# GpSimd additions ordered behind VectorE's in a scheduled attention and expert kernel, with new durations in its build-time scheduler

One core of a Trainium2 chip. The metric is the device time of one execution in microseconds (us), lower is better; a time below is a median over executions.

## The reference

Linear attention with a normalization per head gives a matrix x of 4608 rows by 512. Four experts follow, each a two-layer network with a ReLU, and their outputs are added with a weight per row. Everything is float32. Shortened:

```python
kv = einsum('bhsd,bhse->bhde', k, v)          # 8 batches, 8 heads, 576 rows, 64 columns
out = einsum('bhsd,bhde->bhse', q, kv)
x = out / sqrt(mean(out*out) + 1e-6) * g_norm # then laid out as 4608 x 512
p = domain_probs / (domain_probs.sum(-1, keepdims=True) + 1e-09)
for e in range(4):                            # w1: 512 x 1024, w2: 1024 x 512
    h = np.maximum(x @ w1[e], 0.0)
    out += p[:, e:e + 1] * (h @ w2[e])
```

## The kernel before

The rows go in nine blocks; a block and an expert make a stage, 36 in all. "Up" is x @ w1 with two nested levels of Strassen's scheme (7 products instead of 8, 49 in all), "down" is h @ w2, with one level or, in 18 "deep" stages, two. Strassen saves matmuls and costs additions. Those of PSUM banks are on VectorE and ScalarE; those of SBUF tiles ("port sums") may run on VectorE or on GpSimd:

```python
def combine(key, cost, out_, a, b, op, reads, writes):
    plan.add(
        key, cost,
        lambda eng: adder(eng).tensor_tensor(out=out_(), in0=a(), in1=b(), op=op),  # L337
        reads=reads, writes=writes, port=True,
    )
```

No order is written down. While the program is built, a list scheduler (`Plan.layout`) runs through a model of the core, with a duration for every operation. It decides which engine does a port sum, in which order each engine works, and which buffer a tile gets. It gives the SBUF port to one port sum at a time. A buffer is free again 0.3 us (`CROSS`) after the modelled end of its last use:

```python
op.end = busy[eng] = t + op.cost[eng]
if op.port:
    port = op.end
...
if b.left == 0 and b.kind is not None:
    end = max(o.end for o in [op] + b.readers + b.writers) + self.CROSS
    free[b.kind].append((end, b.slot))
```

On the chip only data and buffer waits remain of this; nothing holds the engines to the model's times. From the second expert on (but for the last stage), a result is added into the output in HBM by a store that GpSimd issues, planned at 0.9 us:

```python
def send(key, i):
    ...
    nc.gpsimd.dma_start(out=dst, in_=cell(i)[parts, :], accum_op=ALU.add)   # L936
    ...
    plan.add(
        key, {"POOL": 0.9 * len(where)} if e and not again else {"SP": 0.55 * len(where)},
        fn, ..., holds=[acc[i // 2]],
    )
```

Of the kernel before, what the change touches and what calls it, by code (L numbers as in the profile page):

```python
# [211 lines left out]
def kernel(  # L212
# [98 lines left out]
    plan = Plan()  # L311

    def pe(products, columns, passes=2):
        return {"PE": passes * products * (2 * columns + 6) / 2400 + 0.003}

    def dve(n):
        return {"DVE": 0.17 + 0.00108 * n}

    def act(n):
        return {"ACT": 0.19 + 0.00088 * n}  # L320

    def either(n):
        return {"DVE": 0.17 + 0.00108 * n, "POOL": 0.1 + 0.0025 * n}

    def gp(n):
        return {"POOL": 0.1 + 0.0025 * n}

    SPC = {"SP": 0.55}

# [64 lines left out]
    def weights_1(e, key, step, need):  # L394
# [11 lines left out]
        def form(k_, o, a, b, op):  # L406
            corner[o] = Buf(None, f"w1c_{e}_{o}")
            combine(
                k_, either(1024), lambda: f[o].ap[:], lambda: f[a].ap[:], lambda: f[b].ap[:], op,
                [f[a], f[b], corner[a], corner[b]], [f[o], corner[o]],  # L410
            )
# [6 lines left out]
        for j, m in enumerate(OUTER):  # L418
            x, low, y = f[m], corner[m], Buf("w1y", f"w1y_{e}_{m}")
            parts = {}  # L420
            for n, (uq, kt) in ((1, (0, 0)), (2, (0, 1)), (7, (1, 0)), (4, (1, 1))):
                parts[n] = (
                    [x, low] if n == 7 else [x],
                    lambda x=x, uq=uq, kt=kt: two(x.ap[:])[:, kt, uq * HN:(uq + 1) * HN],
                )
            for n, at in ((5, 0), (6, 1), (3, 2)):
                parts[n] = ([y], lambda y=y, at=at: y.ap[:, at * HN:(at + 1) * HN])
            for o, a, b, op in (
                (5, 7, 4, ALU.add), (7, 1, 7, ALU.subtract), (6, 5, 1, ALU.subtract),
                (3, 2, 6, ALU.subtract),  # L430
            ):
                combine(
                    need + j / 7, either(HN), parts[o][1], parts[a][1], parts[b][1], op,
                    parts[a][0] + parts[b][0], [low] if o == 7 else [y],
                )
            w1f[e][m] = parts

    def weights_2(e, key, step, deep):
# [9 lines left out]
        def form(k_, o, a, b, op):  # L448
            combine(
                k_, either(1024), lambda: f[o].ap[:], lambda: f[a].ap[:], lambda: f[b].ap[:], op,  # L450
                [f[a], f[b]], [f[o]],
            )
# [37 lines left out]
    def scaled(key, name, raw, n, x):  # L490
# [4 lines left out]
        def rows(b):  # L495
# [6 lines left out]
        )  # L502
        plan.add(
            key, dve(NT),
            lambda eng: nc.vector.reduce_sum(out=ss.ap[0:n, :], in_=rows(sq), axis=AX.X),
            reads=[sq], writes=[ss],
        )

        def power(eng):
# [8 lines left out]
        plan.add(key - 0.3, {"POOL": 1.9}, power, reads=[ss], writes=[ss, rt])  # L518
        plan.add(
            key, dve(NT),  # L520
            lambda eng: nc.vector.tensor_tensor(
                out=rows(x), in0=rows(raw),
# [5 lines left out]
    def attention(b, key, span, rem):  # L528
# [3 lines left out]
        for hp in range(NPAIR):  # L532
# [26 lines left out]
            def turn(eng, bank=bank, qt=qt):  # L559
                for r in range(NR):  # L560
                    rs = slice(r * P, (r + 1) * P)
                    nc.tensor.transpose(bank.ap[:, rs], qt.ap[:, rs], ident[:])  # L562

            plan.add(at(hp), pe(4, P, 1), turn, reads=[qt], writes=[bank])
            plan.add(
                at(hp), act(NT),
# [15 lines left out]
            def diagonal(eng, bank=bank, to=kvbd[hp]):  # L582
                for r in range(2):
                    rows = slice(r * D, (r + 1) * D)
                    nc.scalar.activation(out=to.ap[rows, rows], in_=bank.ap[rows, 0:D], func=ACT.Copy)

            plan.add(at(hp), pe(12, D), key_values, reads=[kt, vt], writes=[bank])
            plan.add(at(hp), {"ACT": 0.5}, diagonal, reads=[bank], writes=[kvbd[hp]])

            raw = Buf("ab" if b else "db", f"raw{n}")  # L590

            def attend(eng, raw=raw, qT=qT, kb=kvbd[hp]):
                for r in range(NR):
                    rs = slice(r * P, (r + 1) * P)
                    nc.tensor.matmul(raw.ap[:, rs], lhsT=qT.ap[:, rs], rhs=kb.ap[:])  # L595

            plan.add(at(hp + 0.4), pe(4, P), attend, reads=[qT, kvbd[hp]], writes=[raw])
            x = Buf("small", f"x{n}")
            scaled(at(hp + 0.4), n, raw, P, x)
# [172 lines left out]
    def up(s, e, views):  # L772
# [16 lines left out]
        for i, m in enumerate(OUTER):  # L789
# [4 lines left out]
            for j, mm in enumerate(ORDER):  # L794
# [28 lines left out]
                def total(a, t, src, add_, whole=whole, key=key):  # L823
                    plan.add(
                        key - 0.4, dve(HN),
                        lambda eng: nc.vector.tensor_tensor(  # L826
                            out=block(whole, a, t), in0=src.ap[:, 0:HN], in1=add_.ap[:], op=ALU.add),
                        reads=[src, add_], parts=[whole],
                    )
# [338 lines left out]
    with tc.manual_schedule(engines={ENG.PE, ENG.DVE, ENG.Activation, ENG.Pool, ENG.SP}):  # L1168
        for i in range(P // D):
            nc.sync.dma_start(out=gcol[i * D:(i + 1) * D, :], in_=g_norm.unsqueeze(1))  # L1170
        make_identity(nc, ident[:])
        nc.vector.memset(mhalf[:], -0.5)
        nc.vector.memset(bd_home[:], 0.0)
        for op in order:
            op.fn(op.eng)


# [26 lines left out]
```

## Time and profile before

| | before |
|---|---|
| median of all its first runs | 1797.2 us (1792.6 to 1798.3) |
| span of the profiled run | 1793.0 us |
| busy TensorE, VectorE, ScalarE, GpSimd | 98%, 66%, 46%, 54% |
| time that is not matmul pace | about 65 us |

A busy share of 98% hides what matters here, since the pace of the matmuls, as the prediction works it out, comes to 1728 us only, and the page counts 1760 as busy. The views to read are the waits of TensorE and the granted clock, which the prediction quotes.

### The profile page before, as it was taken

The numbers are of one execution on the slowest core, as the hardware profiler recorded it, in microseconds if no ns is written. First come the engines' busy times: TensorE is split into PE (matmuls) and PEld (weight loads), VectorE is DVE, ScalarE is ACT, GpSimd is POOL, SyncE is SP. The second block draws the span as 40 slices with busy tenths as digits, with TensorE's granted clock in tenths as the row PEclk, the third lists the DMA queues.
The fourth block names the chain that finished last, engine by engine and source line by source line (L and its number), as shares of the span: only waits on it lengthen the run. The fifth ranks groups of instructions, "written<-read, shape, count | busy, mean of one in ns | idle before, by whom it ended". The sixth has DMA issues, their size and how long they took to land.

```text
span 1793.0 us, 36253 instructions
## 1 busy us (share of the span) xinstructions
PE 1760.0 (98%) x14138; PEld 1683.6 (94%) x14138; DVE 1177.1 (66%) x1909; ACT 815.9 (46%) x1913; POOL 973.0 (54%) x816
## 2 busy tenths in 40 slices
PE   8999999999999999999999999999999999999998
PEld 8899999999989899999999899999999899999997
DVE  5864664556665677777774677777774767777754
ACT  3544544444333345555543345555543345555541
POOL 4945554555335546666546536666555636666520
PEclk9999999999999999999999999999999999999999
DMA  9854544532333334444564334444465334444441
GB/s 238 238 158 145 169 142 124 174 101 112 142 125 107 87 95 111 111 106 106 142 158 118 93 97 106 107 107 107 107 174 135 97 100 107 106 107 107 108 117 36
DMA packets 148587, 220.79 MB, mean 123 GB/s; under 512 B 49600, under 2 KB 90816, under 8 KB 148416
## 3 DMA queue, kind: packets, MB, share of 16 engines
q1 hardware_dynamic: 133312, 191.21, 35.0%
q0 software_dynamic: 15104, 27.27, 10.1%
q8 instruction: 111, 1.82, 0.4%
q14 instruction: 60, 0.49, 0.1%
HBM read 145.30 MB, written 73.14 MB: 122 GB/s over the span
## 4 chain that ended last, share of the span: by engine, by line
PE 84%; POOL 5%; DMA 5%; DVE 3%; issue 2%; ACT 1%; SPq 1%; DVEq 0%; POOLq 0%; ACTq 0%
PE u L802 38%; PE db L966 18%; PE db L1039 9%; PE ab L1039 8%; PE ab L966 6%; DMA out_dram<-big 4%; POOL big L337 4%; DVE big L337 2%; PE ab L595 1%; PE ab L577 1%; POOL out_dram L936 1%; PE ab L605 1%; PE ab L562 1%; SPq L343 1%; DVE big L1072 1%
## 5 line engine op out<-in xcount | busy, mean ns | idle before, releaser
L802 PE MATMUL u<-xf,big 128*128 128x128 f32 x3600 | 494.4, 276 | 0.8 <-ACT snap L818 0.6
L826 DVE TENSOR_TENSOR big<-u,snap 128x256 f32<-128x256 f32 x675 | 280.6, 422 | 305.6 <-PE u L802 201.7
L818 ACT ACTIVATE snap<-u 128x256 f32<-128x256 f32 x756 | 289.6, 384 | 387.9 <-PE u L802 319.8
L802 PEld LDWEIGHTS u<-xf,big 128*128 128x128 f32 x3600 | 456.9, 192 | 9.3 <-ACT snap L818 1.2
L337 POOL TENSOR_TENSOR big<-big,big 128x256 f32<-128x256 f32 (+1 forms) x181 | 295.8, 1638 | 206.5 <-DVE big L337 107.8
L337 DVE TENSOR_TENSOR big<-big,big 128x1024 f32<-128x1024 f32 (+1 forms) x330 | 379.1, 1160 | 32.1 <-ACT big L785 14.5
L802 PE MATMUL u<-xf,w1y 128*128 128x128 f32 x2700 | 381.1, 277 | 11.5 <-DVE big L826 10.3
L802 PEld LDWEIGHTS u<-xf,w1y 128*128 128x128 f32 x2700 | 342.8, 192 | 17.9 <-DVE big L826 11.5
L966 PE MATMUL db<-big,big 128*128 128x256 f32 x1336 | 316.8, 381 | 0.0
L966 PEld LDWEIGHTS db<-big,big 128*128 128x128 f32 x1336 | 242.4, 191 | 26.8
L785 ACT ACTIVATE big<-big 128x1024 f32<-128x1024 f32 x130 | 136.6, 1052 | 20.6 <-DVE big L337 18.1
L936 POOL DMA_DIRECT2D out_dram<-big x98 | 90.3, 1003 | 90.2 <-ACT big L913 45.6
L1064 ACT ACTIVATE snap<-db 128x256 f32<-128x256 f32 x216 | 76.9, 356 | 118.3 <-PE db L1039 105.2
L818 ACT ACTIVATE big<-u 128x256 f32<-128x256 f32 x225 | 86.2, 383 | 95.4 <-PE u L802 84.2
L1072 DVE TENSOR_TENSOR big<-ab,snap 128x256 f32<-128x256 f32 (+1 forms) x204 | 78.8, 386 | 70.9 <-PE ab L1039 40.3
L913 ACT ACTIVATE big<-db,p_all 128x256 f32<-128x256 f32 x96 | 45.5, 474 | 130.2 <-PE db L966 130.2
L337 POOL TENSOR_TENSOR big<-big 128x512 f32<-128x512 f32 (+1 forms) x53 | 74.5, 1406 | 44.5 <-ACT big L785 23.2
L1100 POOL TENSOR_TENSOR big<-big 128x512 f32<-128x512 f32 x17 | 36.2, 2131 | 113.2 <-ACT snap L818 113.2
L337 DVE TENSOR_TENSOR big<-big 128x512 f32<-128x512 f32 (+1 forms) x70 | 93.7, 1342 | 0.2 <-POOL big L337 0.2
L1039 PE MATMUL db<-big,big 128*128 128x128 f32 x648 | 89.8, 275 | 0.0
L920 DVE SCALAR_TENSOR_TENSOR big<-db,p_all,big 128x256 f32<-128x256 f32 x75 | 36.2, 482 | 75.6 <-PE db L966 75.5
L966 PE MATMUL ab<-big,big 128*128 128x256 f32 x360 | 85.8, 384 | 0.0
(198 smaller groups left out, 2682.4 us busy)
## 6 DMA issues: line engine op xcount, KB each, us to landing
xf<-x SPq DMA_DIRECT2D x108, 512.0 KB, 3.7
out_dram<-big POOLq DMA_DIRECT2D x82, 256.0 KB, 5.6
xf<-x_h SPq DMA_DIRECT2D x81, 256.0 KB, 3.1
xf<-x SPq DMA_DIRECT2D x81, 256.0 KB, 3.2
x<-xf SPq DMA_DIRECT2D x36, 512.0 KB, 3.7
big<-in_moe_w_dram SPq DMA_DIRECT2D x31, 512.0 KB, 5.1
small<-in_q_dram SPq DMA_DIRECT2D x72, 128.0 KB, 4.2
kv<-in_k_dram SPq DMA_DIRECT2D x30, 288.0 KB, 3.3
```

The source lines that it names most:

```text
L337: lambda eng: adder(eng).tensor_tensor(out=out_(), in0=a(), in1=b(), op=op),
L785: lambda eng: nc.scalar.activation(out=b.ap[:], in_=b.ap[:], func=ACT.Relu),
L802: nc.tensor.matmul(ps.ap[:, u * P:(u + 1) * P], lhsT=w1f[e][m][mm][1]()[:, u * P:(u + 1) * P], rhs=views[m][mm][1](), start=(mm in (1, 2, ...
L818: lambda eng: nc.scalar.activation(out=where(), in_=ps.ap[:, 0:HN], func=ACT.Copy),
L826: lambda eng: nc.vector.tensor_tensor(out=block(whole, a, t), in0=src.ap[:, 0:HN], in1=add_.ap[:], op=ALU.add),
L913: lambda eng: nc.scalar.activation(out=cell(i, half), in_=ap(), func=ACT.Copy, scale=prob()),
L920: lambda eng: nc.vector.scalar_tensor_tensor(out=cell(i, half), in0=ap(), scalar=prob(), in1=cell(i, half), op0=ALU.mult, op1=ALU.add,),
L936: nc.gpsimd.dma_start(out=dst, in_=cell(i)[parts, :], accum_op=ALU.add)
L966: nc.tensor.matmul(ps.ap[:, 0:HN], lhsT=four(h[m])[:, kt // 2, t, kt % 2, :], rhs=w2f[e][m].ap[:, kt * HN:(kt + 1) * HN], start=(m in (1, ...
L1039: nc.tensor.matmul(ps.ap[:, o * P:(o + 1) * P], lhsT=b.ap[:, col:col + P], rhs=w2q[e][m][mm][1]()[:, kt, :], start=(mm in (1, 2, 5) and o ...
L1064: lambda eng: nc.scalar.activation(out=where(), in_=group_of(ps.ap), func=ACT.Copy),
L1072: lambda eng: nc.vector.tensor_tensor(out=cell(tq, dq), in0=group_of(src.ap), in1=group_of(add_.ap), op=ALU.add,),
```

## The change

The intent: in the model, port sums of VectorE and GpSimd take turns; on the chip, GpSimd runs ahead of the order and holds the port while VectorE needs it. So each GpSimd port sum gets a wait for the last VectorE port sum ahead of it (the "rule"). The scheduler's durations are also set to what the trace shows. All of it:

```diff
     def pe(products, columns, passes=2):
-        return {"PE": passes * products * (2 * columns + 6) / 2400 + 0.003}
+        return {"PE": passes * products * (0.008 + 0.0008125 * columns) + 0.003}
     def dve(n):
-        return {"DVE": 0.17 + 0.00108 * n}
+        return {"DVE": 0.185 + 0.00104 * n}
     def either(n):
-        return {"DVE": 0.17 + 0.00108 * n, "POOL": 0.1 + 0.0025 * n}
+        return {"DVE": 0.185 + 0.00104 * n, "POOL": 0.15 + 0.00225 * n}
     def gp(n):
-        return {"POOL": 0.1 + 0.0025 * n}
+        return {"POOL": 0.15 + 0.00225 * n}
...
+        held = None
         for op in order:
-            op.fn(op.eng)
+            made = op.fn(op.eng)
+            if op.port and op.eng == "DVE":
+                held = made.ins.name
+            elif op.port and op.eng == "POOL" and held is not None:
+                tc.add_manual_dep(made.ins, held, mybir.DependencyInfo(
+                    mybir.DependencyClass.Sync, mybir.DependencyReason.DATA
+                ), reason="SBUF port")
```

## The prediction

> **What bounds the kernel now.** Four experts run over nine blocks of rows, 36 stages; each multiplies by w1 (up) and w2 (down), both by nested Strassen sums, so that VectorE and GpSimd do many additions of SBUF tiles (L337, L1100: "port sums" below) beside TensorE. Deep down stages are those with a second Strassen level. I read the page's busy shares first, then TensorE's waits, then the timeline around the longest of them, then the clock there.
>
> On the page: the span, the busy time of each engine, and the two largest groups of the first matrix product and its eviction.
>
> ```profile
> span 1793.0 us, 36253 instructions
> PE 1760.0 (98%) x14138; PEld 1683.6 (94%) x14138; DVE 1177.1 (66%) x1909; ACT 815.9 (46%) x1913; POOL 973.0 (54%) x816
> ...
> L802 PE MATMUL u<-xf,big 128*128 128x128 f32 x3600 | 494.4, 276 | 0.8 <-ACT snap L818 0.6
> L826 DVE TENSOR_TENSOR big<-u,snap 128x256 f32<-128x256 f32 x675 | 280.6, 422 | 305.6 <-PE u L802 201.7
> ```
>
> TensorE is busy in 98% of the span, so it sets the pace. What matters is how much of its time is not matmul pace. The chain of work shows the pace: 24 passes of 128 columns in 2.68 us (0.1117 us each) and 16 passes of 256 columns in 3.46 us (0.216 us each). The source gives the passes: 36 up stages of 49 products, 2 matmuls, 2 passes are 7056; the 18 deep down stages have 18 x 49 x 2 x 2 = 3528 more of 128 columns; the other 18 have 18 x 14 x 4 x 2 = 2016 of 256; attention and filler add 706 of 128 and 832 of 64 columns (24 in 0.92 us, 0.038 each). So (7056 + 3528 + 706) x 0.1117 + 2016 x 0.216 + 832 x 0.038 = 1261 + 435 + 32 = 1728 us. Of the 1793 us, only about 65 are not pace. That bounds every gain at 3.6%, and head and tail are in it: TensorE is idle 9.1 of the first 100 us, and the last matmul starts 5.4 us before the end.
>
> The waits of TensorE, by what ended them (total us, times, longest), those on VectorE:
>
> ```profile
> PE u L802 <- DVE big L826: 10.5, 6, 3.0
> PE ab L1039 <- DVE big L1072: 6.2, 11, 0.9
> ...
> PE u L802 <- DVE small L826: 0.6, 1, 0.6
> ...
> PE ab L1039 <- DVE small L1072: 0.4, 1, 0.4
> ```
>
> They sum to 10.5 + 6.2 + 0.6 + 0.4 = 17.7 us. L826 and L1072 are the evictions that add a PSUM bank and a snapshot: matmuls wait because VectorE has not emptied a bank. VectorE is busy 66% of the span and its evictions take their normal 0.42 us, so the question is what stood ahead of them. The timeline at the longest such wait (start, duration, engine, line, operation; GpSimd is POOL):
>
> ```profile
> 993.13 1.29 POOL L337 TENSOR_TENSOR kv<-big,kv 128x256 f32<-128x256 f32 x1
> ...
> 996.71 1.11 POOL L337 TENSOR_TENSOR x_rem<-x_rem,small 128x256 f32<-128x256 f32 x1
> ...
> 998.08 1.09 POOL L337 TENSOR_TENSOR x_rem<-small,x_rem 128x256 f32<-128x256 f32 x1
> 1000.19 0.74 DVE L826 TENSOR_TENSOR big<-u,snap 128x256 f32<-128x256 f32 x2
> ...
> 1000.98 1.16 PE L802 MATMUL u<-xf,w1y 128*128 128x128 f32 x4 [3.05 <-DVE big L826]
> ```
>
> and the chain of waits in the same place (start, duration, what):
>
> ```profile
> 993.46 6.81 DVE big L337
> 1000.26 0.68 DVE big L826 x2
> ```
>
> A VectorE sum of 128x1024 took 6.81 us, where the median of its form is 1.22. GpSimd ran eight 128x256 sums from 993.13 without a pause, and the VectorE sum finished only after the last of them; the eviction behind it started at 1000.2 and TensorE stood 3.05 us. The same picture is at 604 and 1405, at the other two changes of expert. Then the clock (us, busy of PE, PEld, DVE, ACT, POOL, granted clock, DMA share, GB/s):
>
> ```profile
> 997.60:1001.00 3.40, 0.35 (x4) 0.16 (x3) 3.33 (x3) 0.75 (x2) 1.57 (x3) 1.00 0.09 37
> 1001.00:1004.50 3.50, 3.50 (x13) 3.14 (x14) 1.82 (x3) 0.00 (x0) 0.00 (x0) 0.51 0.37 117
> 1004.50:1010.00 5.50, 5.50 (x40) 5.19 (x39) 1.48 (x4) 2.46 (x6) 2.58 (x3) 1.00 0.06 22
> ```
>
> After the stall, 3.5 us ran at clock 0.51. The lost time is 3.5 x 0.49 = 1.7 us for each of the three, 5.1 in all. A smaller form comes once in each of 15 deep down stages:
>
> ```profile
> 771.41 4.21 DVE L337 TENSOR_TENSOR small<-big 128x512 f32<-128x512 f32 x1
> ...
> 772.02 2.98 POOL L337 TENSOR_TENSOR big<-big,big 128x1024 f32<-128x1024 f32 x1
> ```
>
> A 0.68 us sum took 4.21, ending 0.6 us after the GpSimd sum of 1024 finished at 775.0. The 11 waits of L1039 on L1072 (6.2 us) follow these.
>
> **What the Trainium skill says.** "SBUF — State Buffer", section "Who interferes with whom": VectorE and GpSimd share one port pair, held as an exclusive lock for a whole instruction; a VectorE operation with two SBUF inputs contends with a GpSimd operation that reads SBUF, and the later one blocks fully. The trace agrees in kind (1.22 becomes 6.81), and goes further: eight GpSimd sums in a row kept VectorE out, so it did not get in between two of them. "GPSIMD Engine Reference", section "Instruction dispatch", puts a two-input body at about 2.5 cycles per element; at the 1.2 GHz that "Trainium Kernel Development and Optimization" gives, 1024 elements would take 2.13 us plus overhead, and the lower half of the trace's 1024 sums takes 2.34 to 2.36. "TensorE: Matmul & The Clock Gate", section "Why this matters for your kernels", warns of TensorE idle gaps over about 3 us between bursts, which drop the clock; the three half-clock stretches in the middle of this run all follow gaps of about 3.1 us. "Perfetto Trace Analysis", section "GPSIMD Engine Instruction", says to time GpSimd by start-to-start spacing: the eight sums are recorded at 1.1 us each but start 0.68 us apart.
>
> **The change, part by part.** It makes every GpSimd sum that uses the port wait for the VectorE sum ahead of it in the build's order. VectorE never waits for GpSimd on this account. So it prevents overtaking, and nothing else. I paired the port sums of the trace with the build order: 735 on VectorE, 618 on GpSimd. 311 of the 618 GpSimd sums started before the VectorE sum ahead of them had ended (144 even before it had started), by 715 us summed, 2.3 on average. The VectorE sums took 135 us more than the medians of their sizes (0.28, 0.42, 0.68, 1.23 us for 128, 256, 512, 1024). In 134 us of this I can name the last GpSimd sum in the way: in 101 it stood later in the order (85 cases), which the change forbids, in 33 earlier (59 cases), which it does not touch. Of the 22 blocks over 2 us, 20 are of the forbidden kind, among them the three long ones and the 15 of 3.5 us.
>
> Gain: 17.7 us of waits plus 5.1 of half clock is 22.8 us; the forbidden kind is 75% of the blocked time (101 of 134) and 91% of the long blocks (20 of 22); I choose 85%, 19 us.
>
> Cost: the 311 sums get later. GpSimd has room: its sums at unblocked pace are 103 x 2.36 + 124 x 1.27 + 316 x 0.73 + 75 x 0.46 = 666 us, with 111 of DMA issue and 83 of the two attention operations 860; the 715 us of waiting, if it all came on top, gives 1575 of 1793. What it makes late was not wanted early, since the order planned it after the VectorE sum; but trains behind a wait can hold the accumulating stores and the attention powers in the same queue. I put 2 us on TensorE for that, an estimate without a row behind it.
>
> The new durations change no work, but reshuffle the order on every engine. The number of port sums stays 1353; GpSimd gets 90, 150, 293, 84 of 1024, 512, 256, 128 (before: 103, 124, 316, 75). At the same pace this is 655 us against 666, and VectorE's sums 612 against 607. Filler in the head falls from 65 to 62 pairs. Neither engine sets the pace, so I count zero with some 5 us of scatter.
>
> Sum: 1796.7 - 19 + 2 = 1780 us, 0.9% less.
>
> **Rivals.** (1) GpSimd becomes the bound: its sums form the weights and inputs of the next stage, and one waiting too long starves TensorE. For: GpSimd already waited 127 us on L337 of VectorE in 45 waits of up to 7.1 us, and would wait more. Against: no wait of TensorE in the trace was ended by a GpSimd sum. It would give 1800 to 1830. (2) The block only changes sides. The new order still has trains of up to seven GpSimd sums between two VectorE sums at the expert changes; started later than before, they can meet the VectorE sum behind them, which has no wait. At 0.68 us each that is 4.8 us again, and a TensorE stall. For: 33 us of such blocks exist now. Against: the order keeps evictions between, paced by TensorE. If it keeps the stalls, 1790 to 1800. (3) All waits on VectorE vanish and more of the small gaps with them: 1796.7 - 23 - 5 = 1769.
>
> **Range and chances.** I predict 1780 us, 1766 to 1793 in 8 of 10. Over 2% faster is below 1760.7, a loss of 36 of the 65 us that are not pace, where I can name 23: 6%. Over 2% slower is above 1832.6 and needs rival 1 in force: 3%. Within 2%: 91%.
>
> **What would show it.** Right: no VectorE sum of 1024 over some 4 us, no 512 of 4.2; TensorE's waits on L826 and L1072 below 4 us together; no half clock at the expert changes; more idle time of GpSimd ended by VectorE's L337. Wrong: TensorE's waits ended by GpSimd sums or by matrix forms, or long VectorE sums with the GpSimd sum ahead of them in the order, or a head longer by several us.

## The result, and the profile after

The changed kernel took 1789.3 us (1788.1 to 1790.1, 4 runs) against 1797.2. The ratio is 0.996, interval 0.9941 to 0.9979. The gain is 7.9 us, where 1796.7 - 1780 = 16.7 was predicted: less than half.

The page after (span, busy time by engine, the same group of evictions; columns as in the prediction):

```profile
span 1786.8 us, 36290 instructions
PE 1753.4 (98%) x14132; PEld 1677.8 (94%) x14132; DVE 1140.3 (64%) x1910; ACT 817.5 (46%) x1913; POOL 831.4 (47%) x815
...
L826 DVE TENSOR_TENSOR big<-u,snap 128x256 f32<-128x256 f32 x720 | 298.7, 421 | 293.1 <-PE u L802 205.0
```

VectorE fell from 1177.1 to 1140.3 us and GpSimd from 973.0 to 831.4. Their work is nearly the same (by the prediction's count 5 us more of sums on VectorE and 11 less on GpSimd), so most of this is blocked time that is gone. Pairing the port sums with the order again, no GpSimd sum of the 617 starts before the VectorE sum ahead of it has ended (before: 311 of 618). But not all blocking is gone. VectorE's port sums still take 86 us more than the medians of their sizes, where it was 135. All of it that can be named is now of the kind that the change doesn't touch, behind GpSimd sums that stand earlier in the order: 85 us in 180 cases, where it was 33. Only one of these is over 2 us. The timeline at the first change of expert that the prediction showed:

```profile
994.20 0.72 POOL L337 TENSOR_TENSOR kv<-kv,small 128x256 f32<-128x256 f32 x1 [1.33 <-DVE big L337]
...
998.40 1.23 DVE L337 TENSOR_TENSOR big<-big,big 128x1024 f32<-128x1024 f32 x1
...
999.76 0.73 POOL L337 TENSOR_TENSOR x_rem<-big,x_rem 128x256 f32<-128x256 f32 x1 [1.43 <-DVE big L337]
```

The GpSimd sums now take 0.72 us instead of 1.1, the VectorE sum of 1024 takes 1.23 instead of 6.81, and the GpSimd sum after it waits 1.43 us for it. TensorE does not stop. Around the three changes of expert (busy of PE, PEld, DVE, ACT, POOL, then clock, DMA share, GB/s):

```profile
600.00:620.00 20.00, 20.00 (x135) 18.74 (x134) 11.48 (x19) 7.75 (x17) 7.68 (x10) 1.00 0.43 106
985.00:1010.00 25.00, 25.00 (x167) 23.35 (x166) 13.60 (x22) 10.35 (x22) 18.58 (x27) 1.00 0.42 110
1395.00:1420.00 25.00, 25.00 (x172) 23.50 (x171) 13.44 (x23) 9.48 (x22) 18.28 (x25) 1.00 0.44 110
```

TensorE is busy throughout at clock 1.00. So the three stalls with their half clock, 14.3 us by the prediction's count (3 x 3.05 + 5.1), are gone as predicted. Where did half of that go? The waits of TensorE (total us, times, longest):

```profile
PE ab L1039 <- DVE big L1072: 10.1, 15, 0.7
PE ab L605 <- DVE small L521: 6.4, 4, 4.7
PE u L802 <- ACT snap L818: 4.7, 9, 1.2
...
PE u L802 <- DVE big L826: 0.9, 2, 0.6
PE u L802 <- DVE small L826: 0.8, 1, 0.8
```

L826 fell from 11.1 to 1.7 us. But L1072 rose from 6.2 to 10.1, with 15 waits instead of 11; waits on the snapshot copies L818 of ScalarE rose from 1.1 to 4.7; and L521, a part of the attention, rose from 2.4 to 6.4, nearly all in one wait of the head (the first 100 us or so, where the attention starts). Together these are (10.1 - 6.6) + 3.6 + 4.0 = 11 us given back, against 11.1 - 1.7 + 5.1 = 14.5 won. That leaves 3.5 of the 6.2 us between the two profiled spans; the rest lies in gaps too short for these rows, and I cannot assign it. The chain of waits in one deep stage (start, duration, what):

```profile
725.66 4.53 DMA out_dram<-big
...
730.28 0.42 DVE big L337
...
732.52 0.42 DVE big L1072
...
732.98 1.16 PE ab L1039 x8
```

A store from `big` to the output lands, and only then can a small VectorE sum run. Behind it VectorE does an eviction L826 and a sum of 1024, which the cut leaves out, and then the eviction L1072, for which TensorE waits 0.70 us. The sum of 1024 in the timeline:

```profile
731.14 1.45 DVE L337 TENSOR_TENSOR big<-big,big 128x1024 f32<-128x1024 f32 x1
```

It takes 0.22 us more than its median of 1.23, beside a GpSimd sum of 0.71 us that started at 730.79. So the port has at most a small part in this wait; the store comes first.

### The profile page after: what moved, and what is told of

The parts are those of the page before. It is cut to its first block, busy times and chain, and to the rows that moved or that the text cites. A ratio compares the mean times of both kernels' runs of the same rounds, so it can differ in the third digit from the quotient of the medians.

```text
span 1786.8 us, 36290 instructions
## 1 busy us (share of the span) xinstructions
PE 1753.4 (98%) x14132; PEld 1677.8 (94%) x14132; DVE 1140.3 (64%) x1910; ACT 817.5 (46%) x1913; POOL 831.4 (47%) x815
## 4 chain that ended last, share of the span: by engine, by line
PE 85%; DMA 6%; POOL 4%; DVE 2%; issue 2%; SPq 0%; ACT 0%; DVEq 0%; POOLq 0%; ACTq 0%
PE u L802 38%; PE db L966 18%; PE db L1039 9%; PE ab L1039 8%; PE ab L966 6%; DMA out_dram<-big 4%; POOL big L337 3%; DVE big L337 1%; PE ab L595 1%; PE ab L577 1%; PE ab L605 1%; POOL out_dram L936 1%; PE ab L562 1%; PE ab L644 0%; DMA out_dram<-small 0%
## 5 line engine op out<-in xcount | busy, mean ns | idle before, releaser
L802 PE MATMUL u<-xf,big 128*128 128x128 f32 x3600 | 503.0, 276 | 5.8 <-ACT snap L818 4.7
L826 DVE TENSOR_TENSOR big<-u,snap 128x256 f32<-128x256 f32 x720 | 298.7, 421 | 293.1 <-PE u L802 205.0
L802 PEld LDWEIGHTS u<-xf,big 128*128 128x128 f32 x3600 | 462.2, 192 | 17.1 <-ACT snap L818 7.5
L337 DVE TENSOR_TENSOR big<-big,big 128x1024 f32<-128x1024 f32 (+1 forms) x377 | 431.3, 1159 | 40.4 <-ACT big L785 15.6
L818 ACT ACTIVATE snap<-u 128x256 f32<-128x256 f32 x756 | 289.5, 384 | 362.1 <-PE u L802 263.8
L802 PE MATMUL u<-xf,w1y 128*128 128x128 f32 x2700 | 378.4, 275 | 0.0
L802 PEld LDWEIGHTS u<-xf,w1y 128*128 128x128 f32 x2700 | 340.4, 192 | 2.1
L337 POOL TENSOR_TENSOR big<-big,big 128x256 f32<-128x256 f32 (+1 forms) x174 | 238.3, 1374 | 151.7 <-DVE big L337 65.0
L966 PE MATMUL db<-big,big 128*128 128x256 f32 x1280 | 302.8, 380 | 0.0
L966 PEld LDWEIGHTS db<-big,big 128*128 128x128 f32 x1280 | 231.3, 190 | 25.3
L818 ACT ACTIVATE big<-u 128x256 f32<-128x256 f32 x240 | 92.1, 384 | 114.6 <-PE u L802 106.8
L337 POOL TENSOR_TENSOR big<-big 128x512 f32<-128x512 f32 (+1 forms) x81 | 95.5, 1184 | 69.0 <-DVE big L337 54.1
L1072 DVE TENSOR_TENSOR big<-ab,snap 128x256 f32<-128x256 f32 x216 | 83.2, 385 | 51.0 <-PE ab L1039 33.8
L337 POOL TENSOR_TENSOR small<-big,small 128x128 f32<-128x128 f32 (+1 forms) x46 | 28.8, 625 | 127.2 <-DVE big L337 68.0
L1039 PE MATMUL db<-big,big 128*128 128x128 f32 x616 | 86.3, 275 | 0.0
L1039 PE MATMUL ab<-kv,big 128*128 128x128 f32 x500 | 74.7, 278 | 10.1 <-DVE big L1072 10.1
```

The source lines that it names most:

```text
L802: nc.tensor.matmul(ps.ap[:, u * P:(u + 1) * P], lhsT=w1f[e][m][mm][1]()[:, u * P:(u + 1) * P], rhs=views[m][mm][1](), start=(mm in (1, 2, ...
L818: lambda eng: nc.scalar.activation(out=where(), in_=ps.ap[:, 0:HN], func=ACT.Copy),
L826: lambda eng: nc.vector.tensor_tensor(out=block(whole, a, t), in0=src.ap[:, 0:HN], in1=add_.ap[:], op=ALU.add),
L966: nc.tensor.matmul(ps.ap[:, 0:HN], lhsT=four(h[m])[:, kt // 2, t, kt % 2, :], rhs=w2f[e][m].ap[:, kt * HN:(kt + 1) * HN], start=(m in (1, ...
L1039: nc.tensor.matmul(ps.ap[:, o * P:(o + 1) * P], lhsT=b.ap[:, col:col + P], rhs=w2q[e][m][mm][1]()[:, kt, :], start=(mm in (1, 2, 5) and o ...
L1072: lambda eng: nc.vector.tensor_tensor(out=cell(tq, dq), in0=group_of(src.ap), in1=group_of(add_.ap), op=ALU.add,),
```

## The experiments

All ten gave correct results. Each was timed in 5 rounds against the kernel before, which had medians of 1795.5, 1796.5 and 1795.5 us in the three jobs. Runs 1 and 2 split the change, and have exactly the instruction order, on every engine, of the kernel before and of the changed one.

### 1. The rule alone

Edit: the loop of the change, without the new durations.

> The rule alone: the durations of before, so each engine's order is that of before, and only the new waits are added. Theory A (the rule is worth what I predicted, and the order that the new durations make gives part of it back): the three stalls of 3.05 us and their half clock (14.3 us together) and most of the 6.6 us of waits on L1072 go, less about 3 us at the head: 1779 us, and the waits of TensorE on L1072 below 2 us. Rival B (the rule takes with one hand and gives with the other: what it makes late in the deep down stages and the head costs TensorE some 8 us, and the order is neutral): 1789 us, as with the whole change, with waits on L1072 of 6 us or more.

Measured: 1778.5 us, ratio 0.9904 (0.9891 to 0.9918). The time is Theory A's, to half a us. But its second half fails. The waits of TensorE and of VectorE in this run, and one VectorE row of its timeline:

```profile
PE ab L1039 <- DVE big L1072: 8.6, 11, 1.2
```

```profile
DVE big L1072 <- DMA out_dram<-big: 51.4, 12, 4.8
```

```profile
773.77 0.42 DVE L1072 TENSOR_TENSOR big<-ab,snap 128x256 f32<-128x256 f32 x1 [4.79 <-DMA out_dram<-big]
```

No VectorE sum of 512 takes over 2.3 us now, and still L1072 holds TensorE up for 8.6 us instead of 6.2. VectorE, freed of its 3.5 us block, arrives earlier and waits 4.79 us for a store. So the port's block was not what bound this place. The profile before had said so. This is its chain of waits at the place that the prediction read in the timeline:

```profile
771.46 6.84 DMA out_dram<-big
...
778.42 0.42 DVE big L1072
...
780.17 1.16 PE ab L1039 x8
```

The store, 6.84 us from issue to landing, releases L1072 at 778.4; the port block ended at 775.6, inside the same wait. What made up for it in run 1: no wait on L826 is left but one of 0.2 us.

### 2. The new durations alone

Edit: the three changed lines of durations, without the loop.

> The new durations alone: each engine's order is that of the changed kernel, without the waits of the rule. Theory A (the order costs): 1802 to 1806 us, with the three stalls at the changes of expert still there and stalls of 0.87 us at L1039 in the 15 deep down stages. Rival B (the order is neutral): 1795 to 1799.

Measured: 1793.5 us, ratio 0.999 (0.9978 to 1.0003). Near Rival B by the time, though the order is not neutral. Its waits of TensorE:

```profile
PE ab L1039 <- DVE big L1072: 10.3, 15, 0.7
PE ab L605 <- DVE small L521: 6.2, 4, 4.5
PE ab L659 <- DVE small L521: 3.2, 1, 3.2
PE u L802 <- DVE big L826: 3.1, 4, 1.1
...
PE u L802 <- ACT snap L818: 1.1, 4, 0.5
```

This order, without any rule, already has short stalls on L826 (3.1 us instead of 10.5, the longest 1.1) and no half clock after the head: the trains (GpSimd sums in a row) are still there, with VectorE sums of 5.2 us at 995 and 1404, but TensorE waits only 1.1 us behind each. The order pays with 10.3 us on L1072, and with waits of 4.5 and 3.2 us in the head. So the long stalls can be removed once only, and the rule had little left to win here: 1793.5 to 1789.3. The waits on the snapshots are 1.1 us here and 4.7 with the rule: those are the rule's, in this order.

### 3. The rule without the head

Edit, on the changed kernel: the wait is made only where `op.key > 1.5`.

> The changed kernel, with the rule left out of the first stage and a half (keys up to 1.5). If the 4.67 us wait of TensorE for the attention power (GpSimd queue held by a sum that waits for VectorE) is the rule's doing, it falls to below 2 us and the time to 1786 us. If it comes from the new order (three VectorE sums of 1024 ahead of the reduction), the wait stays above 4 us and the time at 1789.

Measured: 1798.5 us, ratio 1.0013 (1.0 to 1.0027). A miss. The long wait of the head stays, and a second one comes:

```profile
PE ab L605 <- DVE small L521: 6.2, 4, 4.5
PE ab L659 <- DVE small L521: 3.3, 1, 3.3
```

The first is therefore the order's, as run 2 agrees (4.5). The second, 3.3 us, is one that the rule prevents. The waits on the snapshots are 7.2 us here, and the head has 3.4 us more at half clock, at 75.8. So in this order the rule does two things: outside the head it makes the kernel some 5 us slower (1793.5 in run 2, 1798.5 here, with intervals of the ratios that just touch), and in the head it is worth some 9 us (1798.5 to 1789.3). The timeline of the changed kernel shows the first: a GpSimd sum waits for VectorE, the power (L514) comes after it, then the scaling L521, then the transposes L605:

```profile
56.91 0.73 POOL L337 TENSOR_TENSOR big<-big 128x256 f32<-128x256 f32 x1 [2.63 <-DVE big L337]
...
59.53 1.70 POOL L514 TENSOR_TENSOR rt<-ss,mhalf 128x8 f32<-128x8 f32 x1
...
62.01 1.12 PE L605 MATMUL ab<-ident,small 128*128 128x128 f32 x4 [4.67 <-DVE small L521]
```

Without the wait of the rule at 56.91 the end was the same, so the wait was not what decided it.

### 4. The rule for one kind of sum

Edit, on the kernel before: the rule only where `op.outs[0].kind == "w2y"`, the trains at the changes of expert.

> The order of before, with the rule only for the GpSimd sums that form the second level of w2 (the trains at the changes of expert). If those trains are the whole cause of the three stalls: the stalls and the three half-clock stretches go, 1797 - 14.3 = 1783 us, and the 4.2 us sums of 512 in the deep down stages stay. If something else stalls TensorE there as well, less: 1788 to 1793.

Measured: 1783.1 us, ratio 0.9928 (0.9915 to 0.9941), as expected: the three stalls and half-clock stretches at the changes of expert are gone, L1072 stays at 6.2 us, and a 512 sum of 4.19 us is still there. Of the 4.2 us of waits on L826 that this run keeps, 2.7 are one new wait in the head, at 74.8. So the trains alone are worth 12 us.

### 5 and 6. The landing of the stores in the model

What remained was the store. The scheduler counts it as done 0.9 us after its start, and hands its buffer on 0.3 us later. The page before gives the time to landing (size, median us):

```profile
out_dram<-big POOLq DMA_DIRECT2D x82, 256.0 KB, 5.6
```

The Trainium skill, "Perfetto Trace Analysis", section "DMA Instruction — SWDGE (GPSIMD)", states that the profile of such an instruction ends when its descriptors are made, not when the data has moved. The trace agrees: the instruction takes 0.88 us (median), the landing 5.6. The duration "as traced" was the wrong one to plan a buffer by. Edit, to run 1 (run 5) and to the changed kernel (run 6), after which the model's store ends 6.9 us after its start; the two lines more shift the line numbers of these runs by two:

```diff
                         op.end = busy[eng] = t + op.cost[eng]
+                    if eng == "POOL" and op.kb:
+                        op.end += 6.0
```

> The rule with the durations of before, and the scheduler now counts an accumulating store of GpSimd as done 6 us after its issue instead of at once, so that it does not give the store's buffer to a sum while the store is still reading it. Theory C (the waits of TensorE on L1072 in the deep down stages are VectorE waiting for such a store to land: 12 waits, 51 us, in the run with the rule alone): they fall from 8.6 us to below 2, and the time from 1778.5 to 1771. Rival D (VectorE is late there for another reason, or the buffers are too few, so that the wait moves to another place): 1776 to 1790, with new waits of TensorE elsewhere.

> The changed kernel with the landing of the stores counted in the same way. Theory C: its waits on L1072 (10.1 us) and on the snapshot copies (4.7 us) both follow VectorE sums that wait for a store (30 waits, 41 us), so both go, and the time falls from 1789 to 1776; what then remains against the rule alone is the head (4 us). Rival D: 1785 to 1795.

Measured: run 5 1768.6 us, ratio 0.9849 (0.9835 to 0.9862); run 6 1765.2 us, ratio 0.9831 (0.9817 to 0.9844). Theory C holds, and run 6 went 11 us below its figure. Of its waits of TensorE, the largest and the one on L826 (here L828):

```profile
PE ab L607 <- DVE small L523: 6.4, 4, 4.7
...
PE u L804 <- DVE big L828: 0.9, 2, 0.6
```

VectorE no longer waits for any store in run 6 (41.0 us after the change). Waits on L1072 and on snapshots are gone from its list. By the start-to-start times of the matmuls, TensorE has no gap over 0.25 us from 100 us to the end; such gaps came to 19.9 us after the change, more than the 14.8 of the two rows that Theory C counted. Run 6 beats both kernels, by 1.3% and 1.7%.

### 7 and 8. Which duration

Edit: run 1 with TensorE's new duration only (7), or with those of VectorE and GpSimd only (8).

> The rule with the new duration of TensorE only. If this one makes the order that costs (it moves every product by 3%), 1789 us with 0.87 us stalls at L1039; if it is the sums' durations, 1778.

> The rule with the new durations of VectorE and GpSimd only. The opposite of the run with TensorE's: 1778 us if TensorE's duration makes the costly order, 1789 if the sums' do. Both between 1781 and 1787 if each brings a part, or if any reshuffled order costs about the same.

Measured: run 7 1786.4 us, ratio 0.9952 (0.9939 to 0.9965); run 8 1801.4 us, ratio 1.0032 (1.0018 to 1.0045). Run 7 is near its first case by the time, but its stalls are at L802 and not at L1039; run 8 is outside every case. Either alone costs, and the sums' durations alone cost more than both together. So no one duration is the bad one. Each gives another order, with VectorE's waits for stores in other places. Those of run 8:

```profile
DVE big L826 <- DMA out_dram<-big: 45.7, 17, 3.9
DVE big L1072 <- DMA out_dram<-big: 23.9, 11, 2.9
```

That is 70 us of VectorE waiting for stores, now also ahead of L826. No run counted the landing in these two orders, so it is not shown that the stores made them slow.

### 9 and 10. The landing without the rule

Edit: the two lines added to run 2 (9) and to the kernel before (10).

> The new durations and the landing of the stores, without the rule; against the same with the rule (1765.2 us) this is what the rule is worth once the stores are out of the way. In the run with the durations alone the trains of GpSimd sums stalled TensorE by 1.3 us at two changes of expert and by 3.3 more in the head. If the rule is then worth only that: 1767 to 1770. If the rule does nothing: 1765. If without it the long stalls with half clock return in this order: 1775 to 1780.

> The kernel before with the landing of the stores alone: no rule, old durations. The two causes should add: the stores' 8 us go, the three stalls with half clock (14.3 us) stay: 1797 - 8 = 1789 us, and the difference to the run with rule and landing (1768.6) is the rule's 17 to 20 us. If the landing's new order happens to dissolve the trains too, 1770 to 1778.

Measured: run 9 1779.4 us, ratio 0.9913 (0.99 to 0.9926); run 10 1782.7 us, ratio 0.9937 (0.9922 to 0.9952, with one run of 1790.9 among 1781.6 to 1782.9). Run 9 lies in its third case by the time, but not by its cause: the stalls after the head are of at most 2.05 us, at four places, without half clock. Run 10 lies between its two cases: the new order that the landing makes keeps one of the three long stalls. With these, the eight combinations are complete (median us, and the ratio to the kernel before of the same job):

| | no landing | landing counted |
|---|---|---|
| old durations | 1797.2 (1) | 1782.7 (0.9937) |
| old durations, rule | 1778.5 (0.9904) | 1768.6 (0.9849) |
| new durations | 1793.5 (0.999) | 1779.4 (0.9913) |
| new durations, rule (the change) | 1789.3 (0.996) | 1765.2 (0.9831) |

The runs were in different jobs, so differences between cells are good to 1 or 2 us; the ratios are the safer measure. Without the landing the rule is worth 17 us in the old order (1795.5 in its job, to 1778.5) and 4 to 5 in the new. With it, it is worth 14 to 16 in both (1782.7 to 1768.6, 1779.4 to 1765.2), and the new durations bring 3 to 4 in both. So what spoiled the combination was that the stores' landing was not counted.

## Why the prediction was right or wrong

- **TensorE's pace bounds the kernel, with 65 us beside it: right.** The fastest version still takes 1765.
- **Trains of overtaking GpSimd sums cause the three stalls and their half clock: right.** Run 4 removed those alone and gained 12 us of the 14.3.
- **"The 11 waits of L1039 on L1072 (6.2 us) follow these": wrong.** The port block was real, but lay inside a longer wait for a store. Run 1 removed the block and the waits grew to 8.6. In the changed kernel the waits on L826 and L1072 are 11.8 us together, where the prediction named below 4 as its sign of being right. I had read the timeline there and not the chain of waits.
- **Gain 19 us: about right as a sum, in part by luck.** The rule alone gave 17, and nearly all of it from L826 and the clock, of which I had counted 85%; L1072, which I had counted too, gave nothing. (A recount of the blocks over 2 us finds 21 of 23 forbidden, not 20 of 22: the same share.)
- **Cost of the rule, 2 us: too small in the new order.** The waits on snapshots rose by 3.6 us between run 2 and the changed kernel, and the rule outside the head alone (run 3) left the kernel some 5 us slower than run 2. GpSimd's room was no issue: it is busy 47%.
- **"Neither engine sets the pace, so I count zero with some 5 us of scatter": this step failed.** The new durations moved the rule's 1778.5 to 1789.3, by 10.8 us (10 by the ratios). TensorE's waits on L1072 and on the snapshots rose from 9.6 to 14.8 us, with 30 waits of VectorE for stores, where run 1 has 12 (shorter ones: 41 us in sum, where run 1 has 51). In the head there is a wait of 4.7 us, where there was one of 1.9. A scheduler's durations do not only say how long engines are busy; they say which buffer is handed on when. The rule alone, without another order, came within 2 us of the predicted 1780, which was meant for another kernel.
- **Rivals.** The first came in a mild form, as the head's wait, but runs 2 and 3 lay it to the order. The second came in small pieces, without its stalls: the blocks of the untouched kind grew from 33 to 85 us, but none at the changes of expert stops TensorE. None of the three named the stores.

It stays open why the snapshots are late with the rule in the new order (4.7 us) and in those of runs 7 and 8 (5.8 and 11.9), but not in the old one (1.0). A later issue of the stores fits, since counting their landing removed these waits too (run 6), but no run moved the issue alone. It stays open too that the landing changes the order in other ways than through the buffers; the waits that it removed are those for stores, in both orders.

## What to carry to other kernels

Where a scheduler lays out buffers, the time that it counts for a transfer must be its landing and not the duration of the instruction that issues it. Before a wait is charged to the block that stands in the timeline, the chain of waits at the same place must name it too. A rule that was good in one order is to be measured in the order in which it will run: two remedies for one stall pay once.

## What the Trainium skill lacked or had wrong

- "SBUF — State Buffer", "Who interferes with whom": the lock is described per instruction; what happens when GpSimd has the next sum ready is not said. In the kernel before, 52 VectorE sums that were late by over 0.3 us ended after one GpSimd sum (in one case two) and before the next, already started one by its record; yet three waited for six to eight sums, up to 6.81 us. What sets these apart no run shows.
- "Perfetto Trace Analysis", "DMA Instruction — SWDGE (GPSIMD)": right on the recorded end. No page gives a time for an accumulating store (it would belong to "DMA: Bandwidth & Descriptors"); one of 256 KB from `big` took 0.88 us as an instruction and 5.1 to 5.6 us (medians of the twelve kernels) to landing.
- "TensorE: Matmul & The Clock Gate", "Why this matters for your kernels": its warning of idle gaps over about 3 us fits this kernel only in part. In the kernel before three gaps of 3.09 to 3.21 us (from the starts of the matmuls, less their pace) were each followed by 3.4 us at half clock; one of 3.07 (run 10) and those of 2.05 (run 9) were not. And in run 8 a half-clock stretch of 3.4 us at 1187.1 followed two waits of only 0.79 and 0.99 us; TensorE was busy 1.62 of the 3.40 us before it. So here a gap of 3 us was not needed.
